# A gated recurrence's products on a quarter of the array each: 64x64 corners, v with two tokens per partition

## The chip, the core and the metric

One core of a Trainium2 chip. TensorE (PE) multiplies, VectorE (DVE), ScalarE (ACT) and GpSimd (POOL) do the rest, SyncE (SP) issues most DMAs. The metric is device time in microseconds of one execution.

## The reference

Two blocks, one behind the other. A gated linear recurrence over 4 batches, 8 heads, 768 tokens, head size 48:

```
for t in range(S):
    state = alpha[:, :, t, :, None] * state + einsum('bhd,bhe->bhde', k[:, :, t], v[:, :, t])
    y[:, :, t] = einsum('bhd,bhde->bhe', q[:, :, t], state)
```

Its output, 3072 rows of 384 (8 heads x 48), goes through a router with 8 experts: logits x @ w_gate + log1p(exp(x @ w_noise)) * noise, the two best per row, a softmax over these two, and for each the expert's relu(x @ w1[e]) @ w2[e] (384 to 1024 to 384), weighted and summed. Everything is float32.

## The kernel before

**The recurrence** runs over 24 chunks n of 128 tokens (six to a batch). Heads sit in pairs: pair j (NP = 4) holds heads 2j and 2j+1, each padded from 48 to 64, so that a transposed chunk is 128 partitions (i, d) by 4 pairs by 128 tokens. The pieces of a chunk are functions of `fast_gla`:

- `load`, `load_v`: DMAs of alpha, k, q (three buffers each) and v, tokens on partitions, 48 floats a run.
- `alphas`, `keys`, `queries`: four transposes each on PE; ACT copies alpha and k out, DVE multiplies q with the running product of alpha. `products` and `inverses` are DVE's scans along the tokens; `scaled_keys` multiplies k on POOL. `no_more` checks alpha on ACT.
- `scores`: for each pair and each head i, k against q over 48 partitions; `masked` puts the causal part into `MTs` on DVE (two predicated copies).
- `turn_k`: transposes the scaled keys back. `state`: their product with v, added to the old state on DVE, scaled by `P_end` on POOL. `block`: ACT copies the two heads of a pair into a block-diagonal 128x128 matrix.
- `output`: that block against q for each pair, then v against the masked scores (`add_values`, 48 of 128 columns for each head), all into one PSUM bank; ACT copies it out as `yT`.
- `turn_y`: yT against `to_rows`, a matrix of identity columns and the router's weights side by side, so that one product gives rows of y and logits. `put_y` writes the rows to `x_rows` in DRAM.

A loop over n writes one chunk's worth of these pieces, for different chunks, in the order of a hand-written string, `ORDER`; each engine executes its own in that order. Between them `ROUTE` places the steps of the routing of a unit of six chunks, and `put_some(3)` at a chunk's end issues three of the router's table entries as indirect DMAs on POOL (24 of them for the first two units, which the first expert tiles need).

PSUM has eight banks: two `tp`, two `h`, two scores (`sc0`, `sc1`), one `y`, one `o`. `tp` turns over among the transposes.

The framework gives the DMAs of SP and ACT one of eight semaphores (DMAHW0 to DMAHW7) in turn; one that takes a semaphore again waits first, in its engine's queue, until the earlier DMA with it has landed.

**The experts** follow: 24 tiles of 256 rows, whose two products are written out as a seven-product scheme on half-size matrices at fixed times, then three small tiles. The last chunk's `output` and the last `turn_y` lie inside this stage (`beside`).

A float32 product shows as two MATMUL records and two LDWEIGHTS records in the trace, a transpose as one of each.

## Time and profile before

| | |
|---|---|
| median of three runs | 664.51 us (664.13 to 665.1) |
| profiled execution | 664.91 us, its span 663.2 us |
| PE busy | 646.9 us, 98% of the span |
| DVE, ACT, POOL busy | 458.2, 272.7, 321.2 us |
| recurrence, first output to last but one | 20.94 to 158.17 us |
| granted TensorE clock | 0.996 |

Busy times are the union of an engine's instructions in the span. PEld is PE's weight loading, which overlaps its products. A line such as L461 is a line of the kernel; `x16` counts records.

### The profile page before, as it was taken

Reading aid. Unit: us, or ns where it says so; the run is one execution under the profiler, and the core shown is the slowest. Engines: PE = TensorE matmul, PEld = TensorE weight load, DVE = VectorE, ACT = ScalarE, POOL = GpSimd, SP = SyncE. Lnnn points to the kernel's source line nnn. Section 1 sums busy time; section 2 is a strip of 40 time slices with the busy share of each in tenths; the row PEclk is TensorE's granted clock in tenths of the full one; section 3 lists DMA queues with packets and bytes.
Section 4 is the critical chain, followed back from the end, with each engine's and each line's share of the span. In section 5 each row is a group of like instructions: output and inputs, shape, how many; then the busy total and the mean of one; then the engine's idle time right before and its main releaser. Section 6 shows DMA issues by size and latency. Waiting matters only on the chain. (4 is left out here: it accounts for less than half of the span.)

```text
span 663.2 us, 14823 instructions
## 1 busy us (share of the span) xinstructions
PE 646.9 (98%) x5605; PEld 624.4 (94%) x5605; DVE 458.2 (69%) x1081; ACT 272.7 (41%) x582; POOL 321.2 (48%) x420
## 2 busy tenths in 40 slices
PE   8999999999999999989999999999999999999994
PEld 6898998999999999989999999999999999998894
DVE  6778888877878888766587666576565755647532
ACT  3667667664343334332333432334333343323330
POOL 5362577783445676775424435422554226540332
PEclk9999999999999999999999999999999999999998
DMA  9998997985656757667203476148362483620111
GB/s 142 155 199 162 237 160 143 230 163 179 220 184 213 246 156 225 209 170 257 75 27 124 142 242 239 57 127 299 85 238 67 143 294 90 232 79 8 49 53 49
DMA packets 144180, 105.61 MB, mean 159 GB/s; under 512 B 109255, under 2 KB 131410, under 8 KB 144100
## 3 DMA queue, kind: packets, MB, share of 16 engines
q1 hardware_dynamic: 131716, 80.37, 45.6%
q0 software_dynamic: 12240, 23.80, 12.3%
q8 instruction: 46, 0.75, 0.5%
q10 hardware_dynamic: 144, 0.41, 0.2%
q14 instruction: 34, 0.28, 0.1%
HBM read 94.99 MB, written 14.86 MB: 166 GB/s over the span
## 5 line engine op out<-in xcount | busy, mean ns | idle before, releaser
L936 POOL DMA_INDIRECT x_in<-x_rows,where x48 | 55.2, 1151 | 121.2 <-PE h_ps L1190 65.8
L929 POOL DMA_INDIRECT out_dram<-prev,where x48 | 53.2, 1108 | 64.5 <-DVE prev L1211 44.0
L1183 PE MATMUL sc<-xs,ws 128*128 128x128 f32 x576 | 76.7, 276 | 0.5 <-ACT m L1254 0.5
L1194 ACT ACTIVATE h<-h 128x512 f32<-128x512 f32 x72 | 45.3, 630 | 77.0 <-DVE h L1130 77.0
L921 POOL DMA_INDIRECT prev<-out_dram,where x48 | 55.0, 1146 | 45.0 <-DMA out_dram<-prev,where 22.6
L1183 PE MATMUL sc<-xt,w 128*128 128x128 f32 x576 | 72.3, 275 | 0.4 <-ACT xt L1122 0.4
L1183 PEld LDWEIGHTS sc<-xs,ws 128*128 128x128 f32 x576 | 70.1, 192 | 1.1 <-ACT m L1254 0.7
L1190 PE MATMUL o_ps<-wt,hx 128*128 128x192 f32 x384 | 70.3, 326 | 0.0
L1183 PEld LDWEIGHTS sc<-xt,w 128*128 128x128 f32 x576 | 69.1, 192 | 0.6 <-ACT xt L1122 0.6
L1190 PEld LDWEIGHTS o_ps<-wt,hx 128*128 128x128 f32 x384 | 63.7, 190 | 0.0
L169 POOL DMA_INDIRECT table<-entry,place_u x48 | 55.8, 1162 | 15.5 <-issue 14.8
L1130 DVE TENSOR_TENSOR h<-sc,m 128x512 f32<-128x512 f32 x48 | 33.1, 691 | 38.0 <-PE sc L1183 34.9
L1183 PE MATMUL h_ps<-xt,w 128*128 128x128 f32 x384 | 50.9, 275 | 0.0
L1199 ACT ACTIVATE o<-o_ps,tab 128x192 f32<-128x192 f32 x23 | 9.7, 420 | 96.1 <-PE o_ps L1190 96.1
L396 POOL TENSOR_TENSOR k_P<-k_P,over 128x512 f32<-128x512 f32 (+1 forms) x25 | 28.9, 1158 | 40.2 <-DVE over L378 36.0
L1183 PE MATMUL sc<-xs,w 128*128 128x128 f32 x384 | 46.9, 275 | 0.0
L1183 PEld LDWEIGHTS h_ps<-xt,w 128*128 128x128 f32 x384 | 46.7, 192 | 0.0
L338 PE MATMUL tp<-ident,ins 128*128 128x128 f32 x288 | 44.7, 292 | 1.5 <-ACT shared L351 0.4
L1183 PEld LDWEIGHTS sc<-xs,w 128*128 128x128 f32 x384 | 44.8, 192 | 0.1
L422 DVE COPY_PREDICATED shared<-upto,sc 128x512 f32<-128x512 uint32 x48 | 32.5, 732 | 12.1 <-PE sc L417 12.1
L338 PEld LDWEIGHTS tp<-ident,ins 128*128 128x128 f32 x288 | 33.7, 149 | 6.6 <-issue 1.6
L1190 PE MATMUL o_ps<-w,h 128*128 128x192 f32 x192 | 35.8, 329 | 0.0
(257 smaller groups left out, 1412.0 us busy)
## 6 DMA issues: line engine op xcount, KB each, us to landing
w<-in_moe_w_dram SPq DMA_DIRECT2D x30, 1536.0 KB, 7.5
ins<-in_alpha_dram SPq DMA_DIRECT2D x24, 192.0 KB, 5.0
ins<-in_k_dram SPq DMA_DIRECT2D x24, 192.0 KB, 4.6
ins<-in_q_dram SPq DMA_DIRECT2D x24, 192.0 KB, 5.2
vt<-in_v_dram SPq DMA_DIRECT2D x24, 192.0 KB, 4.4
x_rows<-y_sb SPq DMA_DIRECT2D x24, 192.0 KB, 4.3
ins<-in_moe_w_dram SPq DMA_DIRECT2D x3, 1536.0 KB, 9.4
shared<-in_moe_w_dram SPq DMA_DIRECT2D x3, 1536.0 KB, 6.8
```

The source lines that it names most:

```text
L169: put = nc.gpsimd.indirect_dma_start(out=table, out_offset=bass.IndirectOffsetOnAxis(ap=place, axis=0), in_=entry, in_offset=None, bounds_ ...
L338: nc.tensor.transpose(tp[:, j, :], src[:, 2 * j:2 * j + 2, :], ident)
L396: nc.gpsimd.tensor_tensor(c["k"][:, at], c["k"][:, at], over[:, at, 1:CB], op=ALU.mult)
L422: nc.vector.copy_predicated(MTs[n % 2][:, i], mask_upto, sc)
L921: get = nc.gpsimd.indirect_dma_start(out=rows.bitcast(U32), out_offset=None, in_=out.bitcast(U32), in_offset=bass.IndirectOffsetOnAxis(ap= ...
L929: put = nc.gpsimd.indirect_dma_start(out=out, out_offset=bass.IndirectOffsetOnAxis(ap=at, axis=0), in_=rows, in_offset=None, bounds_check= ...
L936: nc.gpsimd.indirect_dma_start(out=rows, out_offset=None, in_=x_rows[0:units * UT, :], in_offset=bass.IndirectOffsetOnAxis(ap=at, axis=0), ...
L1130: nc.vector.tensor_tensor(to, p, q, op=ALU.add)
L1183: nc.tensor.matmul(bank[name][:, f, :], W[:, ds(f * C, C)], X, start=new and f == 0, stop=True, skip_group_check=True)
L1190: nc.tensor.matmul(bank[name], H[:, f, :], W[:, f, :], start=new and f == 0, stop=True, skip_group_check=True)
L1194: nc.scalar.activation(t, t if src is None else src, AF.Relu)
L1199: nc.scalar.activation(to, src, AF.Copy, scale=gate(i, s))
```

## The change

Every product of the recurrence gets a 64x64 shape, so that it occupies one corner of PE's array: 64 of its rows (partitions of the operands) and 64 of its columns (partitions of the output). Products are written in groups of four, one for each corner (`CORNERS`).

- **Heads by halves.** Pairs 0 and 1 form half hh = 0, pairs 2 and 3 half hh = 1. `k_P` after its transpose is laid out with the tokens of half 0 in 64 columns and of half 1 in the other 64, even and odd tokens apart (c, m): `keys` writes its transposes so (`apart`), and `scaled_keys` follows on POOL in two instructions.
- **v with two tokens per partition**: `load_packed` brings, for each half of the heads, tokens 2m and 2m+1 onto partition m: runs of 96 floats, two DMAs for a chunk in place of one.
- `scores`: 16 products of 48x64 by 128 in place of 8 of 48x128 by 128; `masked` is the same copy with a mask for even and odd tokens, in two pieces that stand apart in the order.
- `state`: 16 products over 64 partitions in place of 8 over 128; its result lies in two banks, and DVE adds it in two instructions.
- `block` and the block matrices go. `before_it` multiplies the old state with q in 8 corner products into the banks `y` and `o`, one chunk ahead; `output` adds v against the scores in 16 products in place of 8. ACT copies yT out in two pieces. In the last two chunks (`APART`) `before_it` is copied out on its own and DVE adds.
- `turn_y`: 16 products of 48x64 by 64 in place of 4 of 128x128 by 112; logits arrive in four parts in place of two (`lgs`), summed by DVE in two steps per unit.
- `to_rows` is half as wide and without zeros; its weights are loaded straight into place by `load_router`, eight DMAs on ACT's queue at the start, in place of four on SP's later with a copy by POOL.
- **Banks**: `ring` takes `tp`, `tp`, `h`, `h` in turn for transposes, state and turn_y.
- **Order**: the transposes of alpha, k, q and the scaled keys stand together, then output, scores, state, before_it, turn_y of one chunk. `put_some` gives two entries a chunk until n = 14, three from n = 15.

```diff
+    def load_packed(src, n, to):
+        for hh in range(2):
+            nc.sync.dma_start(out=to[ds(HC * hh, HC), 0:H // 2 * 2 * D].rearrange("p (h x) -> p h x", h=H // 2),
+                              in_=packed(src, n, hh))
...
+    to_rows = const.tile([C, NP, D + 2 * E], F32, name="to_rows")
+
+    def load_router():
         for w, src in enumerate((moe_w_gate, moe_w_noise)):
             for i, part in enumerate(src.rearrange("(j i d) e -> i d j e", i=2, d=D)):
-                nc.sync.dma_start(out=w_r[ds(DP * i, D), :, w, :], in_=part)
-        return w_r, load_noise(on)
...
+                for hh in range(2):
+                    at = to_rows[ds(DP * (i ^ hh), D), 2 * hh:2 * hh + 2].rearrange("p j x -> p (j x)")
+                    nc.scalar.dma_start(out=at[:, ds(D, 4 * E)].rearrange("p (j w e) -> p j w e", j=2, w=2)[:, :, w],
+                                        in_=part[:, 2 * hh:2 * hh + 2])
...
+    def ring(on, shape):
+        k = turn[0] % 4 // 2
+        turn[0] += 1
+        if k == 0:
+            bank = on["tp"].tile([C, NP, C], F32, tag="tp", name="tp").rearrange("p j t -> p (j t)")
+        else:
+            bank = on["h"].tile([C, FO // 2, C], F32, name="h_ps").rearrange("p f t -> p (f t)")
...
+        CORNERS = [(i, hh) for hh in range(2) for i in range(2)]
+        APART = (NT - 2, NT - 1)
...
-            for j in range(NP):
-                for i in range(2):
-                    r = ds(DP * i, D)
-                    nc.tensor.matmul(c["sc"][i][:, j, :], c["k"][r, j, :], c["q"][r, j, :], start=True, stop=True)
...
+            for jj in range(2):
+                for s in range(2):
+                    for i, hh in CORNERS:
+                        r, j = ds(DP * i, D), 2 * hh + jj
+                        nc.tensor.matmul(c["sc"][i][ds(HC * hh, HC), 2 * jj + s, :], c["k"][r, 2 * jj + s, ds(HC * hh, HC)], c["q"][r, j, :],
+                                         start=True, stop=True)
...
-            nc.vector.tensor_add(S_new, S_old, s1)
...
+            s1 = [ring(on, [C, 2, D]) for hh in range(2)]
+            for jj in range(2):
+                for s in range(2):
+                    for i, hh in CORNERS:
+                        r = ds(HC * hh, HC)
+                        nc.tensor.matmul(s1[hh][ds(DP * i, DP), jj, :], c["k_end"][r, 2 * jj + s, ds(DP * i, DP)],
+                                         c["v"][r, ds(((2 * jj + i) * 2 + s) * D, D)], start=jj == 0 and s == 0, stop=True,
+                                         skip_group_check=True)
+            for hh in range(2):
+                nc.vector.tensor_add(S_new[:, ds(2 * hh, 2), 0:D], S_old[:, ds(2 * hh, 2), 0:D], s1[hh])
...
+            for jj in range(2):
+                for i, hh in CORNERS:
+                    r, j = ds(DP * i, D), 2 * hh + jj
+                    nc.tensor.matmul(y[hh][ds(DP * (i ^ hh), DP), jj, :], Ss[(n - 1) % 2][r, j, :], c["q"][r, j, :],
+                                     start=jj == 0, stop=False, skip_group_check=True)
...
+                            nc.tensor.matmul(y[hh][ds(DP * (i ^ hh), M), jj, :],
+                                             c["v"][r, ds(((2 * jj + i) * 2 + s) * D, M)],
+                                             MTs[n % 2][r, i, 2 * jj + s, :], start=new and jj == 0 and s == 0, stop=True,
+                                             skip_group_check=True)
...
+                            nc.tensor.matmul(banks[r][ds(HC * cc, HC), ds(hh * C + jj * D, PW)],
+                                             yT[half, 2 * hh + jj, ds(HC * cc, HC)], to_rows[half, 2 * hh + jj, :],
+                                             start=hh == 0 and jj == 0, stop=True, skip_group_check=True)
...
-        ORDER = "keys inverses alphas turn_y turn_k scaled queries block output no_more state scores masked products"
+        ORDER = "inverses alphas keys queries scaled turn_k output products scores masked state masked1 before_it no_more turn_y"
...
-                last = [lambda: put_some(3)]
...
+                last = [lambda: put_some(3 if n >= 2 * UC + 3 else 2)]
```

What the orders of the engines make of it, at three places. First PE in one turn of the loop, before: transposes of k (for n + 2) and alpha (n + 3), turn_y of the last chunk (L277), turned keys (L429), transposes of q, then the block product (L461), v against the scores (L254), state (L444), and the scores (L417, eight rows of which two are shown).

```order
L338 MATMUL tp<-ident,ins 128x128 x8
L277 MATMUL h_ps<-to_rows,yT 128x112 x4
L429 MATMUL tp<-ident,k_P 128x128 x4
L338 MATMUL tp<-ident,ins 128x128 x4
L461 MATMUL y<-q_P,S_block_155 128x128 x4
L254 MATMUL y<-shared,vt 48x128 x8
L444 MATMUL o_ps<-vt,k_end 64x48 x8
L417 MATMUL sc_693<-q_P,k_P 128x128
L417 MATMUL sc_694<-q_P,k_P 128x128
```

And after, behind the scores of an early chunk: state (L436), before_it (L456), turn_y (L498), then the next turn's transposes of alpha, k (128x64x2) and q.

```order
L436 MATMUL h_ps<-vt,k_end 64x48 x16
L456 MATMUL y<-q_P,S_157 64x128 x2
L456 MATMUL o_ps<-q_P,S_157 64x128 x2
L456 MATMUL y<-q_P,S_157 64x128 x2
L456 MATMUL o_ps<-q_P,S_157 64x128 x2
L498 MATMUL tp<-to_rows,yT 64x64 x16
L322 MATMUL h_ps<-ident,ins 128x128 x4
L322 MATMUL h_ps<-ident,ins 128x64x2 x4
L322 MATMUL tp<-ident,ins 128x128 x4
```

The corner products follow one another with no whole-array work between, and the two banks that the state's product used (here both h) are the ones that the next chunk's alpha and k are transposed into.

Second, DVE in one turn, before: state's sum, the two masks, the next products' scan, inverses, the query product.

```order
L446 TENSOR_TENSOR S_153<-S_154,o_ps 128x192
L422 COPY_PREDICATED shared<-upto,sc_693 128x512
L422 COPY_PREDICATED shared<-upto,sc_694 128x512
L366 SCALAR_TENSOR_TENSOR P_all<-shared,least 128x516
L368 RECIPROCAL P_all<-P_all 128x4
L378 SCALAR_TENSOR_TENSOR over<-shared,P_all 128x515
L406 TENSOR_TENSOR q_P<-tp,P_all 128x512
```

After:

```order
L410 COPY_PREDICATED shared<-upto,sc_852 128x512
L440 TENSOR_TENSOR S_156<-S_157,h_ps 128x2x48
L440 TENSOR_TENSOR S_156<-S_157,tp 128x2x48
L410 COPY_PREDICATED shared<-upto,sc_853 128x512
L364 SCALAR_TENSOR_TENSOR over<-shared,P_all 128x515
L394 TENSOR_TENSOR q_P<-tp,P_all 128x512
L350 SCALAR_TENSOR_TENSOR P_all<-shared,least 128x516
L352 RECIPROCAL P_all<-P_all 128x4
```

The state's sum, in two instructions, now stands behind the first mask and ahead of the second; the scans stand ahead of the masks.

Third, ACT at the program's start, before: the table load, then the copies of the first chunk's alpha and k.

```order
L1533 UNCONDITIONAL_BRANCH [waits barrier_Pool_Activation_PE_DVE_SP_release]
L351 ACT_TABLE_LOAD [waits DVE_49]
L351 COPY shared<-tp 128x2x128 [waits PE_49]
L351 COPY shared<-tp 128x2x128
L388 COPY k_P<-tp 128x512 [waits PE_49]
```

After (DMAHW0, 1 and 2 are the semaphores of the first chunk's alpha, k and q):

```order
L223 DMA to_rows<-in_moe_w_gate_dram 48x2x8 x4
L223 DMA to_rows<-in_moe_w_noise_dram 48x2x8
L223 DMA to_rows<-in_moe_w_noise_dram 48x2x8 [waits DMAHW0_49]
L223 DMA to_rows<-in_moe_w_noise_dram 48x2x8 [waits DMAHW1_49]
L223 DMA to_rows<-in_moe_w_noise_dram 48x2x8 [waits DMAHW2_49]
L335 ACT_TABLE_LOAD [waits DVE_49]
L335 COPY shared<-tp 128x2x128 [waits PE_49]
```

Eight DMA issues now stand ahead of the table load, three of them with a wait for an earlier DMA's landing.

More of the change, by code (lines that the diff above doesn't have):

```diff
@@ L458, in output @@
                 c = chunks[n]
[L459 to L469 removed]
+                new = "y_ps" not in c
@@ L509, in fast_gla @@
         return (load, load_v, alphas, no_more, products, inverses, keys, scaled_keys, queries, scores, masked, turn_k,
-                state, block, output, turn_y, put_y, route, route_on, all_routed, out_of_range, places)
+                state, before_it, output, turn_y, put_y, route, route_on, all_routed, out_of_range, places)
     def general_gla(es):
@@ L1420 @@
         NOISE_AT = 5
-        FIRST_ORDER = "scores masked inverses keys scaled turn_k queries output block state alphas no_more turn_y products"
-        ORDER = "keys inverses alphas turn_y turn_k scaled queries block output no_more state scores masked products"
+        ORDER = "inverses alphas keys queries scaled turn_k output products scores masked state masked1 before_it no_more turn_y"
+        FIRST_ORDER = "scores masked masked1 inverses keys scaled turn_k queries output state before_it alphas no_more turn_y products"
         def warm(times):
```

276 lines of the change are left out of this document (165 added, 111 removed).

## Prediction

> **What bounds the kernel now.** I read the busy times of the page first, then a table of busy times by stretch, then the order of time on TensorE inside one chunk.
>
> ```profile
> PE 646.9 (98%) x5605; PEld 624.4 (94%) x5605; DVE 458.2 (69%) x1081; ACT 272.7 (41%) x582; POOL 321.2 (48%) x420
> ```
>
> TensorE is busy nearly all the time, so whatever shortens its list of work is worth something; whether another engine then takes its place differs by stage. In the next rows the columns are the stretch, its length, busy us (and instructions) of PE, PE's weight loads, DVE, ACT and POOL, the granted clock, the DMA share and GB/s.
>
> ```profile
> 0.00:10.00 10.00, 7.79 (x26) 5.40 (x26) 6.83 (x15) 3.10 (x5) 6.45 (x32) 1.00 1.11 141
> ...
> 400.00:500.00 100.00, 100.00 (x786) 97.81 (x785) 62.83 (x157) 34.60 (x69) 43.86 (x45) 1.00 0.50 169
> ```
>
> ```profile
> 20.94:158.17 137.23, 134.89 (x1687) 127.03 (x1686) 112.41 (x220) 90.92 (x223) 83.77 (x139) 1.00 0.92 177
> ...
> 95.76:103.19 7.43, 6.42 (x82) 5.97 (x81) 7.33 (x12) 5.47 (x14) 5.97 (x8) 1.00 0.72 129
> ...
> 134.39:140.62 6.23, 6.23 (x82) 5.93 (x81) 4.81 (x8) 4.04 (x11) 5.44 (x7) 1.00 0.74 137
> ```
>
> The stretch 20.94 to 158.17 holds 22 turns of the recurrence's loop: 6.24 us each, PE idle for only 2.34 us in all. The change works here; the expert stage behind it (400 to 500: PE 100 of 100) it hardly touches. In a plain chunk (134.39) DVE has 4.81 of 6.23 us, and in one with routing (95.76) 7.33, where PE already waits. So PE bounds by 1.4 us a chunk and no more: that is what can be had before DVE stands in the way. Now one chunk on PE, start and length of each group; a group's own cost is the distance to the next start.
>
> ```profile
> 140.62 1.06 PE L461 MATMUL y<-q_P,S_block 128*128 128x128 f32 x8
> 141.61 1.09 PE L254 MATMUL y<-shared,vt 128*48 128x128 f32 x16
> 142.53 0.62 PE L444 MATMUL o_ps<-vt,k_end 128*64 128x48 f32 x16
> 143.07 1.16 PE L417 MATMUL sc<-q_P,k_P 48*128 48x128 f32 x16
> 144.17 1.09 PE L338 MATMUL tp<-ident,ins 128*128 128x128 f32 x8
> 145.10 1.04 PE L277 MATMUL h_ps<-to_rows,yT 128*128 128x112 f32 x8
> 145.98 0.60 PE L429 MATMUL tp<-ident,k_P 128*128 128x128 f32 x4
> 146.41 0.60 PE L338 MATMUL tp<-ident,ins 128*128 128x128 f32 x4
> 146.85 1.06 PE L461 MATMUL y<-q_P,S_block 128*128 128x128 f32 x8
> ```
>
> Distances: 0.99, 0.92, 0.54, 1.10, 0.93, 0.88, 0.43, 0.44; sum 6.23. A product is two records (L461: four products, x8), a transpose one. To get the pace of a record I take the last one's length off a group:
>
> ```profile
> L461 PE MATMUL y<-q_P,S_block 128*128 128x128 f32 x192 | 25.4, 275 | 0.0
> ...
> L444 PE MATMUL o_ps<-vt,k_end 128*64 128x48 f32 x320 | 12.8, 224 | 0.0
> ```
>
> ```profile
> L444 PEld LDWEIGHTS o_ps<-vt,k_end 128*64 128x64 f32 x320 | 12.3, 141 | 0.3 <-issue 0.3
> ...
> L461 PEld LDWEIGHTS y<-q_P,S_block 128*128 128x128 f32 x192 | 23.3, 192 | 0.0
> ```
>
> ```profile
> 148.75 0.21 PE L444 MATMUL o_ps<-vt,k_end 128*64 128x48 f32 x2
> ```
>
> L461, one at a time: (1.06 - 0.275)/7 = 0.112 us for 128 columns. L254's sixteen records fill the same 0.92 us that eight would need: two column halves of the array run side by side; L417 shows the same for two row halves. L444 goes in pairs: (0.62 - 0.224)/7 = 0.057 us a pair. Streaming 48 columns needs 48/128 x 0.112 = 0.042; loading 64 weight columns needs 64 x (192 - 141)/64 = 51 ns, so the weight load sets that pace, and two loads run side by side too. The last row says that both records of a pair lie within 0.21 us, less than one's mean length: they start almost together.
>
> **The change, part by part.** *PE, per chunk.* In 64x64 form four records, one for each corner, would run together. Scores: 32 records of 128 columns, eight groups x 0.112 = 0.90 (1.10 now). Output: the same, 0.90 (0.92 now). The product with the old state (before_it): 16 records, four groups, 0.45 (0.99 now, where half of each block is zeros). State: 32 records in eight groups, at the pair's pace 0.057: 0.46 (0.54 now). turn_y: 32 records of 64 columns and 64 weight columns, also 0.057: 0.46 (0.88 now). Sixteen transposes at 0.44/4 = 0.11: 1.76, unmoved. Changes of form: by paces alone today's chunk is 1.76 + 0.90 + 0.90 + 0.46 + 0.90 + 0.78 (L277, 112 columns) = 5.70; the other 0.53 goes to three changes (whole array, columns, rows, whole), 0.18 each. With the transposes together two are left, 0.35. Sum: 0.90 + 0.90 + 0.45 + 0.46 + 0.46 + 1.76 + 0.35 = 5.28, so 0.95 less a chunk. Four at once is not in this trace, only two. The bounds for a group of four: 0.057 (pairs do not disturb each other) and twice a pair's (they go one after the other). I take the first, since rows and columns each double today without a visible loss.
>
> *DVE* keeps its scans, masks and query product. The state's sum is split in two.
>
> ```profile
> L446 DVE TENSOR_TENSOR S<-S,o_ps 128x192 f32<-128x192 f32 x19 | 6.7, 351 | 9.7 <-PE o_ps L444 8.7 <-POOL P_end L407 0.9
> ...
> L682 DVE TENSOR_TENSOR lg<-lgs 128x96 f32<-128x96 f32 x2 | 2.6, 1280 | 0.0
> ...
> L759 DVE TENSOR_TENSOR picked<-picked,h_ps 128x96 f32<-128x96 f32 x2 | 0.5, 234 | 0.0
> ```
>
> Two of 96 elements cost 2 x 0.234 - 0.351 = +0.12: a plain chunk becomes 4.93, still 0.35 under PE's 5.28. The logits' sum gets a second pass, up to 2 x 1.28 per unit of six chunks, +4 us for the two units here. *ACT* loses two block copies and has three more short evacuations: about 4 of 5.3 us, covered.
>
> *POOL* has the table's entries, two a chunk and from the fifteenth chunk three.
>
> ```profile
> L169 POOL DMA_INDIRECT table<-entry,place_u x24 | 28.6, 1193 | 6.4 <-issue 6.0 <-POOL entry L764 0.2 <-POOL S L439 0.2
> ```
>
> With three, POOL is busy 5.44 us (134.39 above) and idles 6.0/22 = 0.3 behind each entry: 6.3 in all, hidden under 6.23 with nothing over and no longer hidden under 5.28. Four chunks at +1.0, of which two chunks' worth of prefetched keys absorb half: +2.
>
> *The sum over the stretch.* PE: 22 x 5.28, less 0.9 in each of three chunks at a batch's end (no state, no turned keys) = 113.5. DVE's routing: 112.41 - (22 x 4.81 - 3 x 0.35) = 7.6, with the logits 11.6; plain chunks hide 0.35 each in the dozen around it, 4 us, so +7. POOL +2; PE's idle time of today stays, +2.3. Together 124.8 for 137.2: **12.4 less**. DVE would then have 112.41 + 19 x 0.12 + 4 = 118.7 of 124.8.
>
> *The start.* The router's weights now go straight into place by eight DMAs on ACT's queue, ahead of ACT's table load and first copy. Three of them wait for the landing of the first chunk's alpha, k and q (rows of the order above).
>
> ```profile
> 0.93 0.44 SPq L195 DMA_DIRECT2D ins<-in_alpha_dram  x1
> ...
> 2.04 0.73 SPq L195 DMA_DIRECT2D ins<-in_q_dram  x1
> ```
>
> ```profile
> DMA to landing us min/median/max: 3.2/3.9/4.8
> ```
>
> ```profile
> L221 SPq DMA_DIRECT2D w_r<-in_moe_w_noise_dram x2: 434/440/445, 17.7 to 18.2; - x2
> ```
>
> ```profile
> 1.68 1.28 ACT L351 ACT_TABLE_LOAD   x1 [1.68 <-DVE shared L307]
> 5.36 0.65 ACT L351 COPY shared<-tp 128x256 f32<-128x256 f32 x2 [2.40 <-PE tp L338]
> ```
>
> ```profile
> 5.77 1.28 DVE L366 TENSOR_TENSOR_SCAN P_all<-shared,least 128x258 f32<-128x258 f32 x2 [0.91 <-ACT shared L351]
> ```
>
> q lands between 2.04 + 3.9 and 2.04 + 4.8, say 6.6; then one issue of 0.44, the table load of 1.28: the first copy at 8.4 where it was at 5.36. DVE's first scan hangs on that copy, and the chain through scan, keys and scores behind it. **+3.0**, between 0 (if the wait were on the issue alone) and 3.5. The loads of chunk 1 wait for router DMAs too; that lies beside it.
>
> *The end.* In the expert stage one output with its block product and two turn_y remain: 0.99 + 0.92 + 2 x 0.88 = 3.67 becomes 0.90 + 0.92 + 3 visits to the corner form at 0.35 = 2.87, where today's one column visit cost 0.18: **-1.0**.
>
> *v and the loads.* v comes in 384-byte rows, half the packets. PE idles 2.34 us in 137, so loads hold nothing up today, and I give it no gain. The profiled run took 664.91 us (span 663.2 and 1.7 around it), 0.4 over the median. 664.9 - 12.4 + 3.0 - 1.0 = 654.5; against the median, **654**.
>
> **The rivals.** *Records can't start closer than today's pairs allow*, 0.057/2 = 29 ns each. Scores, output and before_it (four in 0.112, 28 ns) stay; state and turn_y need 0.91 each: +0.9 a chunk, PE 6.2, which hides DVE's 7 and POOL's 2 again: 22 x 0.9, less 0.45 in the three chunks without a state, less 9, = +9.4: 663.4. For it: no row shows a closer mean; against it: the pair that starts within 0.21 us. The Trainium skill ("TensorE: Matmul & The Clock Gate", section "Wait — 56ns, not 53.3ns?") states a floor of about 25 ns from start to start; as an estimate by that page state and turn_y take 0.8 each and the kernel 660.5. The trace's pairs, 29 ns a record, bear it out as a mean, and the pair that starts together speaks against it as a least distance.
>
> *Two row halves can't write one bank together.* Scores, state, output and turn_y give each row half its own bank; before_it alone lets both write y[hh], on different partitions. Were these serialised: +0.45 x 22, half of it hidden by DVE's routing: 659. Today's L417 uses two banks, so no row tells. The Trainium skill ("TensorEngine Tiling (Array Packing)", section "Gotcha 1: PSUM Pressure") says that different row tiles cannot access the same bank simultaneously.
>
> *DVE becomes the bound by a loop*: the next chunk's first transposes reuse the bank of the state's product, which DVE frees only behind the first mask.
>
> ```profile
> L422 DVE COPY_PREDICATED shared<-upto,sc 128x512 f32<-128x512 uint32 x43 | 29.2, 733 | 9.5 <-PE sc L417 9.5
> ```
>
> From the scores' end DVE needs 0.733 + 2 x 0.234 = 1.2 us, PE's work in between is 0.46 + 0.45 + 0.46 + 0.18 = 1.55. The slack of 0.35 is small: if DVE comes to its mask 0.75 late in each chunk, PE loses 0.4 a chunk, 22 x 0.4 = 9: 663. For it: DVE would be 95% busy; against it: in a plain chunk PE's 5.28 still exceeds DVE's 4.93.
>
> *Loads become the bound, and the kernel slower.* v is now two DMAs, so a chunk issues six, and each waits until the one eight before it has landed.
>
> ```profile
> vt<-in_v_dram SPq DMA_DIRECT2D x3, 192.0 KB, 5.1
> ...
> ins<-in_alpha_dram SPq DMA_DIRECT2D x1, 192.0 KB, 7.0
> ```
>
> A chunk then lasts at least 6/8 of a landing: 5.25 us at 7.0, just under PE's; from 8.3 us on it is 6.23 and the whole gain is gone, while the start's 3 us stay: 667. For it: the DMA share of 0.92 in the stretch, and 1.11 when the queues are full (first row of the table); against it: v's packets halve.
>
> *Corners run only two at a time*: scores and output +0.90 each, before_it +0.45, state and turn_y +0.46 each: 3.2 a chunk, PE 8.4, the kernel near 713.
>
> **How the numbers follow.** Forecast 654, with its own range 648.5 to 658.5: 0.48. Better, about 647, if the start's 3 us and half of the routing hide: 0.07. Spacing, 660 to 664: 0.15. One bank: 0.06. DVE's loop: 0.11. Loads: 0.08. Two at a time: 0.05. Less than 0.2% (1.3 us) can't be told from no change here. Faster: 0.48 + 0.07 + 0.06 + 0.11 of the spacing's + 0.06 of the loop's = 0.78. Same: 0.04 + 0.04 + 0.01 = 0.09. Slower: 0.07 + 0.05 + 0.01 = 0.13. The range leaves out the two slower cases and the edge of the best one: 646 to 664.
>
> **What would show it.** Right: turns of 5.3 to 5.6 us; state and turn_y about 0.5 us each from start to start, before_it under 0.5; ACT's first copy at 8 us or later; DVE over 90% busy from 25 to 150 us. Wrong: 32 records of state in 0.9 us (spacing), before_it at 0.9 (bank), transposes that wait for DVE's sum (loop) or for a DMA (loads), a first copy at 5.4 us (no cost at the start).

## The result

The changed kernel takes 673.66 us (median of four runs, 671.42 to 675.11) where the kernel before took 664.81 in the same session: 1.0128 times as long, 95% interval 1.0095 to 1.0161. Forecast was 654, range 646 to 664. The profiled run took 673.06 us, its span 671.4.

The page of the changed kernel: busy times, TensorE's clock in 40 slices, and the queue that brings instructions (packets, MB, share of the DMA engines).

```profile
PE 636.0 (95%) x7397; PEld 611.8 (91%) x7397; DVE 462.6 (69%) x1109; ACT 262.7 (39%) x608; POOL 340.1 (51%) x440
PEclk9988997989999999998999999999999999999999
q8 instruction: 61, 1.00, 0.6%
```

The last line on the page of the kernel before:

```profile
q8 instruction: 46, 0.75, 0.5%
```

PE has 10.9 us less to do and the kernel is 8 us longer. Its share fell from 98 to 95%, and its clock, full until the end before, has dips in the recurrence. It fetches a third more instructions.

Busy times by stretch of the changed kernel (columns as in the prediction): the same 22 turns, two turns that nothing disturbed, and two windows of 3.41 us, one behind the other.

```profile
19.98:163.94 143.96, 125.40 (x3335) 115.41 (x3337) 115.98 (x243) 81.75 (x244) 101.96 (x159) 0.93 0.84 172
51.42:56.28 4.86, 4.81 (x146) 4.50 (x145) 4.69 (x9) 2.56 (x9) 3.01 (x4) 1.00 0.90 190
84.92:89.84 4.92, 4.92 (x129) 4.64 (x129) 3.90 (x7) 3.32 (x11) 4.50 (x6) 1.00 0.81 162
57.39:60.80 3.41, 2.04 (x73) 1.71 (x68) 3.11 (x9) 3.38 (x8) 2.60 (x4) 1.00 1.23 187
60.80:64.21 3.41, 3.41 (x55) 3.29 (x51) 1.96 (x8) 1.72 (x7) 0.00 (x0) 0.50 0.97 212
```

The stretch went from 137.23 to 143.96 us. An undisturbed turn takes 4.9 us, less than the 5.28 forecast, but the mean is 6.5 (6.24 before): PE idles 143.96 - 125.40 = 18.6 us (2.34 before), and its mean clock is 0.93, a loss of 0.07 x 143.96 = 10.1. The last two rows show how the clock goes: PE was busy for only 2.04 of 3.41 us, and the whole next window ran at 0.50. Such windows begin at 43.73, 60.80, 101.76, 112.00, 132.48 and 146.13; each costs half of 3.41, 1.7 us, six of them 10.2. Without them PE's work is 125.4 - 10.2 = 115.2, against 113.5 in the forecast.

One turn of the changed kernel on PE, in order of time, and what ACT did then:

```profile
66.12 1.05 PE L405 MATMUL sc<-q_P,k_P 48*64 48x128 f32 x32
66.99 0.63 PE L436 MATMUL tp<-vt,k_end 64*64 64x48 f32 x32
67.44 0.28 PE L456 MATMUL y<-q_P,S 48*64 48x128 f32 x1
...
67.90 0.65 PE L498 MATMUL h_ps<-to_rows,yT 48*64 48x64 f32 x32
68.70 1.09 PE L322 MATMUL tp<-ident,ins 128*128 128x128 f32 x8 [0.16 <-DVE S L440]
71.61 0.66 PE L322 MATMUL h_ps<-ident,ins 128*128 128x128 f32 x4 [1.81 <-ACT lgs L507]
```

```profile
67.00 1.28 ACT L821 ACT_TABLE_LOAD   x1
70.45 0.23 ACT L821 ACTIVATE entry<-entry 128x12 f32<-128x12 f32 x1 [2.17 <-DVE entry L815]
```

From start to start: scores 0.87, state 0.45, the product with the old state 0.46, the turn of y at most 0.8 with a wait in it. All four corners run together. Then PE idles 1.81 us: ACT stands at the gates' Exp of the routing until DVE has sorted, and the evacuation of the turned y (ACT's copy of it out of PSUM), queued behind it, holds the bank of the next transposes.

What PE waited for from 20 to 164 us (total, times, longest), the largest of the list:

```profile
PE o_ps L456 <- issue: 4.4, 2, 3.0
PE tp L419 <- POOL k_P L384: 2.0, 2, 1.8
PE h_ps L322 <- ACT lgs L507: 1.8, 1, 1.8
PE tp L322 <- ACT lgs L507: 1.8, 1, 1.8
PE h_ps L322 <- DMA ins<-in_alpha_dram: 1.2, 1, 1.2
PE tp L498 <- issue: 1.2, 1, 1.2
PE y L456 <- ACT yT L484: 1.1, 1, 1.1
PE y L456 <- POOL k_P L384: 1.1, 1, 1.1
```

"issue" is a wait that nothing in the profile releases. The longest of them lies in the middle of one group of products, whose first records had run:

```profile
142.41 0.39 PE L456 MATMUL y<-q_P,S 48*64 48x128 f32 x4
145.85 0.33 PE L456 MATMUL o_ps<-q_P,S 48*64 48x128 f32 x2 [3.04 <-issue]
```

These waits come to 7.0 us in the stretch, in six places; the kernel before has none. They are waits for instructions: each of the six ends 1.3 to 1.6 us behind the landing of a packet of the queue that brings instructions, and such a packet comes only every 5.5 us. For the longest wait it is the packet that ran from 143.31 to 144.25, the only one from 142.80 to 145.86:

```profile
q8 instruction: 1, 0.02, 1.9%
```

By what released them, PE's waits from 20 to 164 us are: instructions 7.0 us, ACT 5.2, POOL 3.1, DVE 1.6, loads 1.2.

The expert stage took as long as before but for 2 us. Its first product (duration minimum, median, maximum; first and last start), before and after:

```profile
L1183 PE MATMUL sc<-xt,w x576: 272/275/377, 161.5 to 643.1; 128*128 128x128 f32 x192
```

```profile
L1285 PE MATMUL sc<-xt,w x576: 272/275/377, 167.6 to 651.6; 128*128 128x128 f32 x192
```

The time of this first product, 161.5 before and 167.6 after, is the yardstick below: in two of the five sessions of experiments the expert stage behind it took about 10 us longer for every kernel, so times of different sessions aren't compared, only ratios to the kernel before in the same session. The yardstick has its own limit. It comes from one profiled execution of each kernel, and executions of one kernel differ by several us: acts_moved below took 667.6 us in the profiled one and 673.3 in the median of ten. Differences of less than about 5 us in it prove nothing.

### The profile page after: what moved, and what is told of

It is laid out like the page before. It is cut to its first block, busy times and chain, and to the rows that moved or that the text cites. A ratio compares the mean times of both kernels' runs of the same rounds, so it can differ in the third digit from the quotient of the medians.

```text
span 671.4 us, 18637 instructions
## 1 busy us (share of the span) xinstructions
PE 636.0 (95%) x7397; PEld 611.8 (91%) x7397; DVE 462.6 (69%) x1109; ACT 262.7 (39%) x608; POOL 340.1 (51%) x440
## 5 line engine op out<-in xcount | busy, mean ns | idle before, releaser
L1023 POOL DMA_INDIRECT prev<-out_dram,where x48 | 53.5, 1115 | 43.7 <-DMA out_dram<-prev,where 20.8
L171 POOL DMA_INDIRECT table<-entry,place_u x48 | 58.7, 1223 | 15.1 <-issue 14.7
L384 POOL TENSOR_TENSOR k_P<-k_P,over 128x256 f32<-128x256 f32 x48 | 40.9, 878 | 23.0 <-ACT k_P L374 15.6
L364 DVE TENSOR_TENSOR_SCAN over<-shared,P_all 128x515 f32<-128x515 f32 (+1 forms) x25 | 29.6, 1187 | 9.6 <-POOL k_P L384 9.5
L410 DVE COPY_PREDICATED shared<-upto,sc 128x512 f32<-128x512 uint32 x48 | 34.3, 729 | 2.5 <-PE sc L405 2.1
L350 DVE TENSOR_TENSOR_SCAN P_all<-shared,least 128x516 f32<-128x516 f32 (+1 forms) x25 | 31.6, 1266 | 5.6 <-ACT shared L335 3.0
```

The source lines that it names most:

```text
L171: put = nc.gpsimd.indirect_dma_start(out=table, out_offset=bass.IndirectOffsetOnAxis(ap=place, axis=0), in_=entry, in_offset=None, bounds_ ...
L350: nc.vector.tensor_tensor_scan(P_all[:, at], a_alls[n % 2][:, at], least.rearrange("p j t -> p (j t)")[:, at], 0.0, op0=ALU.mult, op1=ALU.max)
L364: nc.vector.tensor_tensor_scan(over.rearrange("p j t -> p (j t)")[:, hi - 1:lo:-1], a_alls[n % 2][:, hi:lo + 1:-1], c["P_all"][:, hi:lo + ...
L384: nc.gpsimd.tensor_tensor(k_P[:, jj], k_P[:, jj], inverse[:, jj], op=ALU.mult)
L410: nc.vector.copy_predicated(MTs[n % 2][:, i].rearrange("p (a s) t -> p a (s t)", a=2), mask_upto, chunks[n]["sc"][i].rearrange("p (a s) t ...
L1023: get = nc.gpsimd.indirect_dma_start(out=rows.bitcast(U32), out_offset=None, in_=out.bitcast(U32), in_offset=bass.IndirectOffsetOnAxis(ap= ...
```

## Experiments

"Issue" is the sum of PE's waits without a releaser, "idle" is 144 us less PE's busy time, both from 20 to 164 us. In seven rows from light_dve to few_quiet the ratio has no interval: it comes from one execution. These seven kernels leave out or replace work, and their values are not those of the computation.

| kernel | first expert product | issue | idle | clock | ratio to before |
|---|---|---|---|---|---|
| before | 161.5 | 0 | 2.7 | 1.00 | 1 |
| after | 167.6 | 7.0 | 18.6 | 0.93 | 1.0128 (1.0095 to 1.0161) |
| acts_moved | 163.3 | 9.3 | 18.8 | 0.96 | 1.0077 (1.0035 to 1.0118) |
| puts_two | 171.0 | 10.9 | 20.0 | 0.94 | 1.0141 (1.0058 to 1.0223) |
| acts_puts | 169.0 | 8.4 | 18.0 | 0.95 | 1.0106 (1.0041 to 1.0172) |
| acts_rank | 166.0 | 7.6 | 19.9 | 0.94 | 1.0049 (1.0004 to 1.0093) |
| light_dve | 170.3 | 14.2 | 20.3 | 0.93 | 1.005 |
| light_acts | 168.0 | 14.7 | 22.6 | 0.98 | 1.001 |
| spaced | 184.5 | 10.4 | 13.1 | 0.96 | 1.017 (1.0074 to 1.0266) |
| no_traffic | 169.1 | 5.1 | 18.8 | 0.94 | 1.001 |
| quiet | 161.7 | 6.0 | 18.9 | 0.98 | 0.998 |
| quiet_light | 160.2 | 3.3 | 14.7 | 0.94 | 1.044 |
| few_records | 163.9 | 0.4 | 20.8 | 0.98 | 0.997 |
| few_quiet | 163.6 | 1.4 | 20.9 | 0.95 | 0.999 |
| hybrid_so | 170.7 | 1.1 | 17.1 | 0.98 | 1.0122 (1.0012 to 1.0233) |
| hybrid_acts | 165.7 | 1.3 | 8.9 | 0.95 | 1.0006 (0.9966 to 1.0046) |

**What a wait costs in clock.** Into the kernel before I put eight pauses, each a product that waits for a run of ACT copies:

```
+        PAUSE = {4: 4, 5: 8, 12: 4, 17: 8, 18: 4, 19: 12, 20: 8, 21: 12}
+        def pause(count):
+            for _ in range(count):
+                nc.scalar.copy(late, ones)
+            nc.tensor.matmul(on["y"].tile([C, NP, C], F32, tag="y", name="y")[:, 0, :], ones, late, start=True, stop=True)
```

> The kernel before the change, with eight pauses of TensorE: at the end of eight turns a product waits for a run of 4, 8 or 12 small ACT copies (estimate from ACT's 0.18 to 0.25 us for one: about 0.8, 1.7 and 2.6 us). Theory (a wait of 1 us and more inside one 3.4 us window halves the clock of the next): windows of half clock appear behind most of the pauses from 1.7 us on, and the span grows by the sum of the pauses plus 1.7 us for each such window: with about 13 us of pauses and five windows, 664.9 becomes 686. Rival (the 64x64 products themselves lower the clock): no window at half clock, and the span grows by no more than the pauses, 678 or less.

Its group of products, two of the pauses in order of time, and the windows around the first of them:

```profile
L1430 PE MATMUL y<-late,ones 128*128 128x128 f32 x16 | 5.4, 430 | 20.1 <-ACT late L1429 20.1
```

```profile
50.43 0.72 PE L1430 MATMUL y<-late,ones 128*128 128x128 f32 x2 [1.55 <-ACT late L1429]
155.53 0.49 PE L1430 MATMUL y<-late,ones 128*128 128x128 f32 x2 [1.05 <-ACT late L1429]
```

```profile
47.13:50.54 3.41, 1.85 (x29) 1.48 (x26) 2.59 (x5) 2.37 (x7) 1.51 (x3) 1.00 0.79 148
50.54:53.95 3.41, 3.41 (x17) 3.41 (x18) 2.23 (x3) 1.17 (x2) 0.97 (x1) 0.50 1.27 194
```

The pauses sum to 20.1 us, not 13, and the span grew from 663.2 to 695.8, by 32.6. The other 12.5 are the clock: seven of the eight pauses, all but the one of 1.05 us, were followed by half clock, in eight windows. The theory's price of up to 1.7 us a window holds, in a kernel without a single 64x64 product, so the rival (the form itself lowers the clock) isn't needed. Its limit of 1 us does not hold: the pause of 1.05 us cost nothing more.

**Many small products or few long ones.** Two kernels add about 2 us of unused PE work to each of 19 turns of the kernel before, behind the state's product:

```
+            for _ in range(36):   # many_small
+                nc.tensor.matmul(o_ps[0:HC // 2, 380:381], ident[:, 0:HC // 2], ident[:, 0:1], ...)
+            for _ in range(6):    # few_long
+                nc.tensor.matmul(o_ps[:, 192:384], ident, S_old.rearrange("p j d -> p (j d)"), ...)
```

> The kernel before the change, with 36 one-column products of 32 columns' weights behind each turn's state product (results unused): 72 more records a turn, so 154 where there were 82, as many as in the changed kernel. Estimate from the closest mean spacing in the trace before, 28 ns a record: 2.0 us more in each of 19 turns, +38: 703. Theory (TensorE uses its instructions up faster than they are fetched): on top of that, waits of 0.4 to 1.5 us that no semaphore ends and that end about 1.4 us behind an instruction fetch, in at least a third of the turns, and half-clock windows behind some: 8 us and more over the added work itself. Rival (the changed kernel's waits come only from ACT, POOL and banks): no such wait; TensorE's idle time in the stretch stays at 2 to 3 us.

> The kernel before the change, with six 192-column products behind each turn's state product (results unused): 12 more records of 0.168 us a turn, 2.0 us of work, with hardly more instructions. Both theories: +38, 703, turns of 8.3 us, TensorE never idle and no half-clock window in the stretch. It is the control for the run with many small products: same added work, a sixth of the instructions.

few_long did as expected: its first expert product came 37.6 us later, with turns of 8.38 us and the clock at 1.00 from 20 to 164 us. many_small did not. It has no wait without a releaser, yet its first expert product came at 239.5, 78 us later. The group of its small products from 20 to 164 us, and two consecutive windows:

```profile
L448 PE MATMUL o_ps<-ident 128*32 128x1 f32 x932 | 31.9, 171 | 0.0
```

```profile
106.87:110.28 3.41, 3.41 (x80) 3.27 (x79) 1.27 (x5) 0.64 (x3) 2.08 (x9) 1.00 0.85 160
110.28:113.69 3.41, 3.41 (x19) 3.41 (x18) 3.34 (x5) 1.74 (x4) 0.00 (x0) 0.50 0.89 134
```

PE is busy in every microsecond, and still the window behind the one with the one-column products runs at half clock. So here the clock does not follow PE's busy time as the profile counts it. That it follows how much work the array does, so that records that move one column count like idleness, is the nearest reading; no further run tests it. The run says nothing for or against the supply of instructions: at 10.2 us a turn it used them up more slowly than the changed kernel.

**Taking away one wait at a time.** ACT's routing steps were moved behind the output's evacuation (Exp, Ln and the gates' Exp apart), and the table entries set to two a chunk:

```
-        STEPS = ((1, 1), (1, 6), (1, 12), (2, 1), (2, 4), (2, 12), (3, 4), (4, 3), (4, 4))
+        STEPS = ((1, 1), (1, 8), (2, 8), (2, 12), (2, 14), (3, 1), (3, 4), (3, 8), (3, 14), (4, 8), (4, 10))   # acts_moved
+        STEPS = ((1, 1), (1, 8), (2, 8), (2, 12), (2, 13), (3, 1), (3, 4), (3, 8), (3, 14), (4, 14), (4, 15))  # acts_puts
+        STEPS = ((1, 1), (1, 8), (2, 8), (2, 12), (2, 13), (3, 1), (3, 4), (3, 8), (3, 14), (5, 8), (5, 10))   # acts_rank
-                last = [lambda: put_some(3 if n >= 2 * UC + 3 else 2)]
+                last = [lambda: put_some(2)]                                       # puts_two, acts_puts, acts_rank
```

> Theory (new waits of TensorE, each with a price in clock): ACT's table loads for the routing stand ahead of the evacuations that free TensorE's banks. With Exp, Ln and the gates' Exp moved behind the output's evacuation, the four waits at 59.35, 69.80, 99.48 and 109.86 us (1.13 + 1.81 + 1.12 + 1.81 = 5.9 us) go, and with them the half-clock windows at 60.80, 101.76 and 112.00 (1.7 us of work lost in each, 5.1): the profiled 673.06 becomes about 662. Rival one (supply of instructions is the only limit): the waits come back as waits for instructions, 669 to 673. Rival two (the 64x64 form itself lowers the clock): windows of half clock stay where they are, and only the 5.9 us go: 667.

> Two table entries a chunk throughout in place of three from the fifteenth chunk on. Theory: POOL holds TensorE up only at 129.29 (1.78 us) and causes one half-clock window behind it (132.48, 1.7 us): 673.06 becomes about 669.6. Rival (POOL alone explains the loss): a whole table entry of 1.2 us less in each of four chunks takes away 5 us and more: 668 or less. Rival (supply of instructions): no change, 672 to 673.

> The changed kernel with ACT's routing steps behind the output's evacuation, the rank product two thirds of a turn later behind POOL's counts, and two table entries a chunk throughout. Theory (ACT, POOL and supply each hold TensorE up): what is left are the waits for instructions and their half-clock windows, 664 to 668. Rival (supply alone): waits for instructions take the place of the others, 669 to 674.

> The changed kernel, all of its computation and traffic, with ACT's routing steps behind the output's evacuation, the rank product a chunk later and two table entries a chunk. If ACT and POOL are relieved and only the supply of instructions is left short: first product of the expert stage at 159 to 163, 0.995 to 1.005 of the kernel before. If the supply takes back what ACT and POOL give: 164 to 168 and 1.005 to 1.013.

In acts_moved the four waits named are gone (the trace puts the one of 1.12 us down to POOL, not ACT) and half-clock windows are three in place of six (0.96), but others stand in their place, much as the first rival has it (1.0077 of 664.8 is 669.9, and the theory had 662):

```profile
PE tp L498 <- issue: 2.8, 1, 2.8
PE h_ps L498 <- DVE picked L841: 2.7, 1, 2.7
PE h_ps L860 <- POOL past L853: 2.0, 1, 2.0
PE o_ps L456 <- issue: 1.9, 2, 1.2
```

The wait for POOL comes from the edit: the rank product had come too close behind POOL's counts, which acts_rank mends. Fewer table entries gave nothing. All four kernels stay at 18 to 20 us of idle time. Against the changed kernel acts_moved gives back half a per cent, with overlapping intervals, and acts_rank 0.8, with intervals that just don't overlap. acts_puts was to reach 664 to 668; 1.0106 of 664.8 is 671.8, inside its rival's 669 to 674. acts_rank meets its first forecast by the ratio and its second by the yardstick, so it doesn't decide between them.

**Is it DVE?** With 116 us of work in the stretch against PE's 115 it might set the pace. One of its two masks is left out, so that half of the scores is not used:

```
-            if n < NT:
+            if n < NT and i == 0:
                 nc.vector.copy_predicated(MTs[n % 2][:, i]...
```

> The changed kernel without the second of DVE's two masks in each turn (that half of the scores is not used, its factors stay zero): 0.73 us less of DVE's 5.3 a turn, nothing else changed. If DVE, with 116 us of work in the stretch against TensorE's 115, sets the pace and every other wait only shifts: first product of the expert stage from 167.6 to 157 to 160. If supply, ACT and POOL are the loss and DVE only waits along: 165 to 168.

> All records and all data traffic, ACT's and POOL's routing moved (166.0 alone), and one mask less on DVE: what is left is the supply of instructions. Its cost is the difference to the run without traffic. If DVE sets the pace: 155 to 159, waits without a releaser of 5 to 8 us still there. If the supply alone sets it: 163 to 167.

It does not. With 12 us less on DVE the stage got no shorter, where 7 to 11 us were forecast; the waits without a releaser doubled, to 14.2 and 14.7 us. The largest in light_acts:

```profile
PE tp L322 <- issue: 3.5, 3, 1.7
PE o_ps L456 <- issue: 2.9, 4, 1.5
PE h_ps L322 <- issue: 2.2, 1, 2.2
```

In these two runs PE waits for its own instructions in place of the rest. It is not so everywhere: in acts_rank, with ACT and POOL relieved, PE waits 9.3 us for DVE and 7.6 for instructions.

**What makes the instructions late?** Two kernels take away one side each. few_records replaces the 80 records of state, old-state product and turn of y by 12 long ones; no_traffic stops the loads (an earlier version, no_loads, let the check on alpha write zeros into the kept buffers, so that the kernel repeated its work at the end; it took 2339.49 us, and only its first part can be read).

```
+                nc.tensor.matmul(s1[hh], c["k_end"][:, 2 * hh, :], ...)            # few_records: 2 products for 16
+                nc.tensor.transpose(y[hh][:, jj, :], Ss[(n - 1) % 2][:, ds(2 * hh, 2), :]..., ident)   # 4 for 8 products
+                nc.tensor.transpose(banks[r][:, ds(hh * C, C)], yT[:, 2 * hh + r, :], ident)          # 4 for 16
```

```
-  load(n + 5, "a"), load(n + 4, "kq")
+  load(n + 5, "a" if n < 5 else ""), load(n + 4, "kq" if n < 5 else "")   # no_loads; no_traffic also reuses v from n = 9
```

> From the fifth turn on alpha, k and q of later chunks are not loaded (the three rotating buffers keep older values), so these loads' traffic is gone from the stretch. If TensorE's instruction fetches are late because the data's packets are in their way: the waits that no semaphore explains (0.76 + 0.43 + 1.20 + 3.04 us behind 75 us, and the window at 146.13) go, 5 us or more: 667 or less. If TensorE simply uses up its instructions faster than a fetch takes: they stay, 671 to 674. If loads of data were the bound after all: every turn falls to about 5.3 us and the time to 655.

> The changed kernel with the same stages, waits and data traffic, but the state's product, the product with the old state and the turn of y replaced by 4 full-array records each of about the same length (the values are then not those of the computation): 68 records fewer a turn, of 152, at nearly the same TensorE time. Theory (supply of instructions): the waits without a releaser go from 20 to 164 us (8 us in the changed kernel), the half-clock windows behind them too; the waits for ACT and POOL stay or grow a little: 658 to 666. Rival (the rate of instructions has nothing to do with it): waits without a releaser stay at 6 us and more, 670 to 676.

> The changed kernel without the loads of alpha, k and q from the fifth turn on and of v from the ninth chunk on (buffers keep older chunks' values; the check on alpha writes beside them, so that they stay valid). Same instructions on TensorE, a fifth of the data traffic behind 60 us. If the data's packets are what makes the instruction fetches late: behind 60 us no wait without a releaser, and 5 us and more less: 660 to 668. If a fetch is too slow for this rate of instructions by itself: waits without a releaser of 5 us and more in the stretch, as before, 669 to 676.

Instruction and data packets from 20 to 164 us: the changed kernel, few_records, no_traffic.

```profile
q1 hardware_dynamic: 79844, 23.59, 80.3%
q8 instruction: 26, 0.43, 1.3%
```

```profile
q8 instruction: 16, 0.26, 0.8%
```

```profile
q1 hardware_dynamic: 26264, 12.05, 33.1%
q8 instruction: 26, 0.43, 1.3%
```

26 packets for 6,679 records of PE: 257 each. few_records needs 16 and waits 0.4 us without a releaser in place of 7.0: the corner form's rate of records is needed for these waits. no_traffic needs as many packets as the changed kernel; one wait of 2.1 us lies at 42 us, before the loads stop, and behind it none is longer than 0.43 and none ends 1.3 to 1.6 us behind a packet. no_loads has 2.6 us of them, all before 44 us.

Data traffic goes with more of these waits but is not needed for them. Three pairs of runs differ in the loads alone (and in where the check on alpha writes): 7.0 and 5.1 us (after, no_traffic), 7.6 and 6.0 (acts_rank, quiet), 14.7 and 3.3 (light_acts, quiet_light), one execution each. Yet in quiet, without loads, a wait of 1.30 us ends at 108.00, again 1.35 us behind an instruction packet, and from 104.80 to 106.70, before and while this packet came, there was one packet of data on the loads' queue:

```profile
108.00 0.32 PE L440 MATMUL h_ps<-vt,k_end 64*64 64x48 f32 x6 [1.30 <-issue]
```

```profile
q8 instruction: 1, 0.02, 2.9%
q1 hardware_dynamic: 1, 0.00, 0.6%
```

quiet_light has one of 1.13 us at 106.26 that is like it. Nor does an instruction packet take longer beside traffic: 1.16 us in the mean from 60 to 164 us in the changed kernel, 1.23 in quiet. Why one comes too late and the next does not stays open.

Neither run got the time back. few_records idles 20.8 us, now for DVE, ACT and POOL, and no_traffic 18.8. By the yardstick the times forecast for them (658 to 668, there 152 to 163) were missed, at 163.9 and 169.1; their ratios of 0.997 and 1.001 would allow them, in a session in which the kernel before spread from 676 to 690 us.

**More room between the bursts.** Eight idle transposes between scores and state:

```
+            for bank in wide:
+                for j in range(4):
+                    nc.tensor.transpose(bank[:, ds(j * C, C)], ident, ident)
```

> The changed kernel, with eight idle transposes of the identity between the scores and the state (overwritten by the state's product): 0.88 us of work, 16 instructions and about 0.3 us for the changes of form a turn, in 19 turns +22 us of TensorE work. Theory (supply of instructions, then the clock): the fetches catch up while the transposes run, the waits that end with a fetch and the half-clock windows mostly go, turns lie near 6.2 us without the outliers of 7.4 to 10.2, and the time rises by 8 or less: 673 to 681. Rival (the 64x64 form itself lowers the clock, or ACT's and POOL's waits have nothing to do with TensorE's pace): half-clock windows stay, and the work comes on top: 690 to 696.

By the yardstick it lost 16.9 us for about 22 of added work, where the theory allowed 8, and idle time fell only to 13.1; its ratio, 1.017 with a wide interval, is 676 of 664.8 and would still fit the theory's time. Its statement on the waits failed: those without a releaser stayed, at 10.4 us, with one of 3.9. So 1.2 us of room a turn is not enough for the instructions to catch up.

**All reliefs together.** quiet is no_traffic with acts_rank's edits, few_quiet is few_records with them, quiet_light is quiet with one mask less.

> The changed kernel with all its records, but with the three reliefs together: no loads of alpha, k, q and v behind the first chunks (older values stay in the buffers), ACT's routing steps behind the output's evacuation with the rank product a chunk later, two table entries a chunk. Read by the first product of the expert stage (161.51 us in the kernel before, 167.58 in the changed one), since the expert stage's own length differs between chips. If supply, ACT and POOL with the half clock behind them are the whole loss: 6 + 6 + 2 us of waits and five of six windows of 1.7 us go, 144 to 150. If other waits take their place (DVE's sum, the keys on POOL): 156 to 164.

> The kernel with 68 records fewer a turn (state, product with the old state and turn of y as full-array products; values not those of the computation) at full data traffic, with ACT's routing steps moved, the rank product a chunk later and two table entries a chunk. There waits without a releaser were already gone and the first product of the expert stage lay at 163.9. If what was left are ACT's four waits, POOL's turns of 6.77 us with three entries, and the half clock behind them: 7 + 6 + 1.7 less, 148 to 152. If DVE or POOL's scaled keys bound the turns anyway: 156 to 163.

> The three reliefs (no loads behind the first chunks, ACT's routing steps moved, two table entries a chunk), which alone gave 161.7, and one mask less on DVE. If DVE was the further bound: 150 to 154 and TensorE's idle time from 20 to 160 us at 8 us or less. If the waits have yet another cause: 158 to 162, idle time 15 us and more.

The stretch from 20 to 164 us in quiet_light, the most relieved:

```profile
20.00:164.00 144.00, 129.34 (x3466) 119.94 (x3466) 108.81 (x239) 85.60 (x255) 105.17 (x163) 0.94 0.42 110
```

Only 3.3 us are waits for instructions, but 14.7 us of idle time and 0.06 of the clock remain. None of the first theories' sums (144 to 150 for quiet, 148 to 152 for few_quiet, 150 to 154 for quiet_light) came: 161.7, 163.6 and 160.2. What is left in quiet and quiet_light are scattered waits for DVE (11.2 and 9.6 us, the longest 3.7 and 3.4), some with a half-clock window behind them; in few_quiet PE waits 11.5 us for loads, 7.3 of them v's. Which of them a further relief would bring to an end stays open. (quiet_light's ratio of 1.044 comes from its end, where PE is busy for 21 of the last 49 us; its values differ, so that end can't be compared.)

**Only two products in corners.** Scores, output and state go back to halves of the array, v to plain rows:

```
-                for s in range(2):
-                    for i, hh in CORNERS: ...                      # scores, state, output
+                for i in range(2): nc.tensor.matmul(..., c["k"][r, j, :], c["q"][r, j, :], ...)
-        ORDER = "... output products scores masked state ..."
+        ORDER = "... output state products scores masked ..."
```

> Only the product with the old state and the turn of y stay in 64x64 form (they brought most: 0.99 to 0.45 and 0.88 to 0.5 us a turn); scores, output and state go back to halves of the array, v to plain rows, POOL's scaling to one instruction, and the state stands beside the output: 112 records a turn in place of 152. From the kernel before: 6.23 - 0.54 - 0.38 + 0.18 for one more change of form = 5.5 us a turn. Theory (supply, with ACT and POOL beside it): half or less of the waits without a releaser, 0.98 to 0.995 of the kernel before (651 to 661 against 664.8). Rival (the waits come from the routing on ACT and from POOL alone, whatever the records): 4 waits of 1 to 2 us with three half-clock windows as in the changed kernel, and no wait without a releaser.

> The same, with ACT's routing steps behind the output's evacuation, the rank product later and two table entries a chunk throughout. Theory: the waits of 1 to 2 us for ACT and POOL go as well, and with the supply no longer short TensorE idles under 6 us in the stretch: 0.975 to 0.985 of the kernel before (648 to 655 against 664.8). Rival (supply alone decides): the same time as without these moves, within 0.3%.

As the supply theory has it, the waits without a releaser fall to 1.1 and 1.3 us. Both forecasts of the time were missed (0.98 to 0.995, and 0.975 to 0.985). In hybrid_so waits for v's load (3.4 us), ACT's copies (8.5) and q's load (2.3) take their place. hybrid_acts has the lowest ratio of the versions with right values, and equals the kernel before. Its first eight turns take 5.6 us each (6.4 before); later turns of 6.1 and four half-clock windows use that up. No version with right values beats the kernel before.

## Why the prediction was wrong

Against the forecast for the profiled run, 654.5, 673.06 is 18.6 more. In the stretch 143.96 - 124.8 = +19.2; the start -4.0; the expert stage and its beginning +3.4.

The 19.2 in the stretch are three parts. PE's work is 115.2 for 113.5 (+1.7), its idle time 18.6 for 7 + 2 + 2.3 = 11.3 (+7.3), and the half clock 10.2 for nothing (+10.2).

- **The clock was put at nothing**, and it is the largest part: 10.2 us, from six windows at 0.50, each behind a window in which PE idled for 1.37 us or more. Two of them follow waits for instructions (43.73, 146.13), four follow waits for ACT or POOL. The trace before has no such window in the recurrence, and its longest single wait there is 1.0 us; the pauses show 1.05 us without the effect and 1.55 with it. The prediction carried no row on how a wait in PE changes its clock.
- **"PE's idle time of today stays, +2.3"** failed too. The forecast took DVE's routing and POOL's entries as two sums of overhang (+7, where its own 11.6 - 4 is 7.6, and +2), called ACT covered, and gave every other wait its old length. Measured are 5.2 us of waits for ACT and 7.0 for instructions, with 1.6 for DVE and 3.1 for POOL. An undisturbed turn of PE is 4.9 us and DVE's work 5.3 a turn in the mean, so there is little slack for a wait of 1 to 2 us on any engine; that is an argument. What the runs show is that relief moves the waits and does not end them: with ACT, POOL or DVE relieved, idle time stayed at 18 to 23 us, in acts_rank with more waits for DVE and in light_acts with more for instructions. Why the sum stays stays open.
- **A term was missing: the supply of instructions**, the 7.0 us of these waits. The forecast counted records by their time only. The stretch holds 3335 of them where there were 1687, each with its weight load, in a time that was to be shorter; no row of before shows a wait for instructions, and none was asked for.
- **POOL**: the scaling was left at its old cost inside 5.44. It is 1.75 us a chunk (two of 0.878) where it was 1.19, as the rows of the changed kernel's page show:

```profile
L384 POOL TENSOR_TENSOR k_P<-k_P,over 128x256 f32<-128x256 f32 x48 | 40.9, 878 | 23.0 <-ACT k_P L374 15.6
L171 POOL DMA_INDIRECT table<-entry,place_u x48 | 58.7, 1223 | 15.1 <-issue 14.7
```

  PE waits 3.1 us for it in the stretch. No run mends the scaling alone; puts_two, which takes other work off POOL, gained nothing.
- **The start, +3.0**, did not come, though its mechanism is there: the router's DMAs and the first chunk's loads hold ACT's table load until 5.67 and its first copy to 6.97 (5.36 before, 8.4 forecast).

```profile
5.67 1.28 ACT L335 ACT_TABLE_LOAD   x1 [5.67 <-DMA to_rows<-in_moe_w_gate_dram]
6.97 0.65 ACT L335 COPY shared<-tp 128x256 f32<-128x256 f32 x2
```

  The first output starts at 19.98, where the first turn of before began with its block product at 19.95: the later copy did not delay it. What does set that time was not followed.
- **The end, -1.0**: the stage behind 167.6 took 503.8 us in place of 501.7, with one half-clock window at 303.
- **Right were PE's work** (115.2 without the slow windows, 113.5 forecast), four corners at once (state 0.45, old state 0.46, both forecast at 0.45 to 0.46; a turn even 4.9) and DVE's busy time (115.98 against 118.7). No run tests v's rows alone. The rivals on spacing, on the bank and on corners two at a time fall with the same rows. The rule behind the first, a floor of about 25 ns from start to start (the Trainium skill, "TensorE: Matmul & The Clock Gate", section "Wait — 56ns, not 53.3ns?"), does not hold across corners: 32 records in 0.45 us are 14 ns each. The rule behind the second (the Trainium skill, "TensorEngine Tiling (Array Packing)", section "Gotcha 1: PSUM Pressure") doesn't show as time here: both row halves wrote one bank in 0.46 us.

In number the outcome was nearest to the rivals of loads (667) and of a loop over DVE (663), but by chance. Neither happened: in the stretch PE waits 1.2 us for loads and 1.6 for DVE, and neither rival had a price for the clock.

## What to carry to other kernels

A form that cuts the work per instruction must be costed in instructions as well: at about twice the records a microsecond (23 for 12), PE waited for instructions, which it did not before. When an engine's list of work shrinks to the length of its neighbours', its idle time is a new unknown; take the neighbours' longest single waits (here an Exp whose input another engine still sorted), not their averages. And give a stretch of 3.4 us in which PE idles for about 1.4 us or more a second price, half such a window at half clock: here six of seven were followed by it.

## What the hardware showed beyond that

PE's clock is halved in whole windows of 3.41 us. In the changed kernel six of the seven windows of the stretch in which PE was busy for 2.04 us or less halved the next one. The seventh, 67.63 to 71.04 with 2.00 us, did not, though it holds most of the wait of 1.81 us shown above. Over all the runs with half-clock windows, many_small aside, PE busy for 1.50 us or less of a full-clock window between 20 and 164 us always halved the next and 2.53 or more never did; in between both occur. In many_small even windows that are 100% busy with one-column products in them are followed by half clock. The Trainium skill ("TensorE: Matmul & The Clock Gate", section "What's actually happening") has the half clock after at least one idle window of about 3.4 us; the length agrees, the condition doesn't.

One fetch of instructions is 16 KB for about 257 records of PE. In the changed kernel one comes every 5.5 us (26 in 144), and at this rate waits of up to 3.0 us appear that no semaphore ends and that end 1.3 to 1.6 us behind such a fetch. At 16 in 144 us one wait of 0.4 us is left (few_records) and one of 1.4 (few_quiet), neither of them that close behind a fetch.
